# One more pair of input buffers and two more output buffers in the last stage of an attention and two-layer MoE kernel on one core

## The chip, the cores and the metric

The kernel runs on one core of a Trainium2 chip. The metric is the device time of one execution in microseconds (us), the median of the executions shown. Beside it stands one execution taken with the hardware profiler; all rows below come from that one. PE is the matrix engine, PEld its weight loads, DVE the vector engine, ACT the scalar engine, SP the engine that issues nearly all transfers; SPq is its queue.

## The reference, cut to what matters

```python
p_packed = sm_attn(p, k, v)               # 8 x 8 heads, 576 tokens, head size 64, 32 packed rows
out = sm_attn(q, p_packed, p_packed)
x  = out, heads merged                    # 4608 tokens x 512
h  = (x @ w1) * (x @ w2) @ w3             # 512 -> 1024 -> 1024
x2 = h @ w_out                            # 1024 -> 512
g  = leaky(x2 @ moe2_w_in)                # 512 -> 2048, max(0.01 h, h)
y  = g @ moe2_w_out                       # 2048 -> 512
```

All is float32. The kernel computes each large product in three passes: every operand is split into a high part that the matrix engine takes exactly and a low rest, and high x high, high x low and low x high are added in PSUM.

## The kernel before, in words

The first part, up to about 604 us, does the attention and the first MoE layer and leaves x2 in DRAM. The change is in the part behind it, the last stage, which does g and y with Strassen's scheme in Winograd's form: a product of 2 x 2 blocks is made from seven block products instead of eight, and each operand is therefore needed in seven sums of its blocks, its "forms", every one as a high and a low part.

The stage runs over 18 tiles, numbered t (`TB`). The 2048 middle columns are cut into three parts F of width 3, 3 and 2 (`PARTS`, the `n` below), and each part runs over six blocks of 768 tokens (`NB`); t counts through the six blocks of F = 0, then of F = 1, then of F = 2. For a tile:

- `load_forms` (line 664) fetches the seven forms of x2 of that token block from the DRAM buffer `xfd`, two transfers of 384 KB for each, into tiles with the tags `xh` and `xl`. Each tag has `XF` buffers, used in turn. The first four forms of tile t + 1 stand in the program ahead of the output work of tile t - 1, the other three behind it.
- `h_unit` makes x2 @ w_in: for the forms in the order 1, 2, 6, 5, 7, 4, 3, and for each of the n column chunks, 6 matmuls of 384 columns (line 750). So a form is 18 matmuls where n is 3 and 12 where it is 2. The sums in PSUM are taken out by ACT copies (line 710), DVE additions (line 713) and the leaky activation (line 698). PSUM has three banks called b, three c, two a.
- `g_ops` makes the forms of g with ACT casts (line 540) and DVE subtractions (lines 536, 125).
- `begin_o` takes four output tiles with the tag `o`, which has `OB` buffers; for F > 0 it loads the partial result of the part before into each (line 802, 384 KB).
- `o_unit` makes g @ w_out for the tile before, adds into the `o` tiles (lines 708, 713; ACT copies at line 710 where F is 0) and stores the four of them (line 821) to `part` or, for F = 2, to `out`.
- Where a part ends, the weight forms of the next are made: `make_wi` (loads at line 654) and `load_wo` / `make_wo` (line 691), with casts and subtractions at the same lines 540, 536 and 125.
- In tiles 0 to 3 the forms of x2 for the token blocks behind are made beside it (`stage_b`, loads at line 554, stores at 558).

Instructions of one engine run in the order in which they stand in its queue, and a transfer that waits for its buffer holds all that is behind it on SPq. That order isn't written by hand here: the program is planned when it is built, with a simulated timeline (line 891). A transfer's place on SPq, and how the matmuls of `h_unit` and `o_unit` are interleaved, come from when the plan thinks that buffers and operands are ready. Other counts of buffers can so change the order of all engines in this stage.

The pools `b1` (with `xh`, `xl`) and `b2` (with `o`) lie in SBUF where the tiles of the first part lay.

Of the kernel before, what the change touches and what calls it, by code (L numbers as in the profile page):

```python
# [57 lines left out]
def tile_kernel(ctx, tc, qT, kT, vL, pT, w12, w3b, wo1, win, wo2, out):  # L58
# [573 lines left out]
    PARTS = ((0, 3), (6, 3), (12, 2))  # L632
    TB = 3 * NB
    ORDER = (1, 2, 6, 5, 7, 4, 3)
    XF, XR, XT, GR, GS, GH, GL, OB = 4, 5, 2, 5, 2, 5, 5, 4
    wi = {m: b1.tile([P, 2, 2, 384], F32R, name=f"wi{m}") for m in ORDER}

    def form_w(w, size):
# [256 lines left out]
```

## Time and profile before

| what | before |
|---|---|
| median of 3 executions | 1335.64 us (1331.0 to 1338.62) |
| the profiled execution | 1334.15 us |
| its span, first to last instruction | 1332.4 us |
| last stage, first matmul to the end of the span | 604.3 to 1332.4, 728.1 us |
| PE busy, whole span | 1264.0 us (95%) |
| DVE / ACT busy, whole span | 908.5 us (68%) / 623.9 us (47%) |
| transfers, whole span | 283.10 MB, mean 212 GB/s |
| mean granted clock of PE | 0.986 of full speed |

The profiled execution stands 1.5 us below the median and 1.75 us above its own span; a sum that is made in the trace is added to 1334.15. An idle time in the trace is written behind the instruction that ended it, as [idle <- releaser]. Where several things were waited for, the one named is the last by the profile.

### The profile page before, as it was taken

To read this page: it belongs to the slowest core of one execution; us is meant where nothing else is said; L and a number is where in the kernel's file an instruction comes from. 1 tells how busy PE (TensorE), PEld (TensorE's weight loads), DVE (VectorE), ACT (ScalarE), POOL (GpSimd) and SP (SyncE) were. 2 spreads that over 40 slices of the span, in tenths; PEclk is the share of its full clock that TensorE was granted. 3 is DMA by queue.
4 is the path that set the end of the run, shared out by engine and by line. 5 is a ranking of instruction groups with operands and counts; after the bars stand their busy time and mean duration, and the time that the engine had idled before them with its cause. 6 is when DMAs were issued, how large, how long until landed. Compare 5 with 4: busy or idle time off the path is not lost.

```text
span 1332.4 us, 23526 instructions
## 1 busy us (share of the span) xinstructions
PE 1264.0 (95%) x9048; PEld 1187.1 (89%) x9048; DVE 908.5 (68%) x1455; ACT 623.9 (47%) x1165; POOL 138.6 (10%) x105
## 2 busy tenths in 40 slices
PE   5658999999999999999999999989999999999998
PEld 3446989898888989799999999989999999899997
DVE  7999546576767678835867853856576459486667
ACT  4435343545454555535655654645433344344432
POOL 7874101110110101000000000000000000000000
PEclk9779999999999999999999999999999999999999
DMA  9636125384847464626887886366645764878874
GB/s 359 244 125 217 57 77 190 110 292 144 276 147 256 150 223 157 230 99 226 276 316 259 289 287 207 117 237 214 213 149 185 235 213 136 287 257 303 297 288 154
DMA packets 139377, 283.10 MB, mean 212 GB/s; under 512 B 14849, under 2 KB 66049, under 8 KB 139265
## 3 DMA queue, kind: packets, MB, share of 16 engines
q1 hardware_dynamic: 130048, 272.16, 60.1%
q10 hardware_dynamic: 9216, 9.44, 2.1%
q8 instruction: 71, 1.16, 0.4%
q14 instruction: 42, 0.34, 0.1%
HBM read 202.38 MB, written 79.17 MB: 211 GB/s over the span
## 4 chain that ended last, share of the span: by engine, by line
PE 74%; DMA 11%; DVE 8%; issue 3%; POOL 1%; SPq 1%; ACT 1%; POOLq 0%; ACTq 0%; DVEq 0%
PE mm L120 26%; PE b L750 25%; PE c L750 13%; PE a L750 6%; DMA xh<-xfd 4%; PE at L153 3%; DVE cT L269 2%; DMA xl<-xfd 1%; DVE cT L272 1%; DMA part<-o 1%; DMA wi<-wid 1%; PE at L211 1%; DMA xfd<-P 1%; POOL c L279 1%; DMA v<-vL 1%
## 5 line engine op out<-in xcount | busy, mean ns | idle before, releaser
L120 PEld LDWEIGHTS mm<-AT,M 128*128 128x128 f32 x1536 | 207.1, 188 | 31.4 <-issue 10.7
L750 PE MATMUL b<-xh,wi 128*128 128x384 f32 x768 | 219.4, 338 | 11.3 <-DMA xh<-xfd 5.6
L120 PE MATMUL mm<-AT,M 128*128 128x288 f32 x1536 | 223.2, 300 | 5.0 <-DVE W L125 2.3
L750 PE MATMUL b<-gh,wo 128*128 128x384 f32 x768 | 213.8, 335 | 1.4 <-DVE o L713 1.4
L120 PEld LDWEIGHTS mm<-ab,W 128*128 128x128 f32 x1536 | 203.9, 188 | 7.8 <-ACT x2s L455 4.2
L120 PE MATMUL mm<-ab,W 128*128 128x288 f32 x1536 | 207.6, 295 | 0.0
L750 PEld LDWEIGHTS b<-xh,wi 128*128 128x128 f32 x768 | 141.6, 189 | 14.2 <-ACT gr L710 6.1
L750 PEld LDWEIGHTS b<-gh,wo 128*128 128x128 f32 x768 | 140.3, 188 | 2.2 <-issue 1.0
L750 PE MATMUL b<-xl,wi 128*128 128x384 f32 x384 | 129.3, 337 | 0.1
L750 PE MATMUL b<-gl,wo 128*128 128x384 f32 x384 | 128.4, 334 | 0.0
L279 POOL TENSOR_TENSOR c<-cT,c 128x512 int32<-128x512 int32 x56 | 77.1, 1378 | 347.1 <-DVE cT L272 191.2
L750 PE MATMUL c<-gh,wo 128*128 128x384 f32 x384 | 107.3, 336 | 0.8 <-DVE o L708 0.8
L540 ACT CAST gh<-gr 128x1152 fp32r<-128x1152 f32 (+1 forms) x72 | 75.7, 1052 | 69.1 <-PE b L750 32.2
L750 PE MATMUL c<-xh,wi 128*128 128x384 f32 x384 | 106.4, 336 | 1.5 <-DMA xh<-xfd 1.5
L125 DVE TENSOR_TENSOR gl<-gr,gh 128x1152 fp32r<-128x1152 f32 (+1 forms) x72 | 87.7, 1223 | 23.4 <-ACT gh L540 23.3
L120 PE MATMUL mm<-ab,w 128*128 128x512 f32 x192 | 57.1, 454 | 40.8 <-DVE W L125 14.7
L434 DVE TENSOR_TENSOR ab<-mm,a 128x288 f32<-128x288 f32 x128 | 57.7, 453 | 50.2 <-PE mm L120 33.6
L120 PEld LDWEIGHTS mm<-ab,w 128*128 128x128 f32 x192 | 41.0, 220 | 56.1 <-DVE W L125 15.3
L540 ACT CAST gh<-gs 128x1152 fp32r<-128x1152 f32 (+1 forms) x54 | 56.9, 1054 | 61.4 <-PE b L750 32.7
L125 DVE TENSOR_TENSOR ab<-ab,ab 128x288 fp32r<-128x288 f32 x124 | 61.3, 496 | 35.5 <-ACT ab L439 33.7
L698 ACT ACTIVATE gr<-gr 128x1152 f32<-128x1152 f32 (+1 forms) x54 | 57.3, 1062 | 46.0 <-DVE gr L713 45.7
L439 ACT CAST ab<-ab 128x288 fp32r<-128x288 f32 x128 | 55.1, 432 | 45.3 <-DVE ab L434 45.1
(123 smaller groups left out, 2155.4 us busy)
## 6 DMA issues: line engine op xcount, KB each, us to landing
xh<-xfd SPq DMA_DIRECT2D x126, 384.0 KB, 5.4
xl<-xfd SPq DMA_DIRECT2D x126, 384.0 KB, 5.0
part<-o SPq DMA_DIRECT2D x48, 384.0 KB, 2.9
o<-part SPq DMA_DIRECT2D x48, 384.0 KB, 4.2
c<-wo SPq DMA_DIRECT2D x19, 512.0 KB, 5.1
xfd<-xt SPq DMA_DIRECT2D x49, 192.0 KB, 3.2
xfd<-xr SPq DMA_DIRECT2D x49, 192.0 KB, 3.4
raw<-kT SPq DMA_DIRECT2D x32, 288.0 KB, 5.3
```

The lines of the kernel that those rows point to most:

```text
L120: ins = nc.tensor.matmul(dst, lhs(i), rhs(j), start=first and n == 0, stop=last and n == 2)
L125: engine.tensor_tensor(out=out, in0=x, in1=rd(hi), op=ALU.subtract)
L153: ins = nc.tensor.matmul(dst(h)[c * 32:c * 32 + 32], lhs[r, c, :], rhs(c)[r], start=True, stop=True)
L211: ins = nc.tensor.matmul(ps[r, :64], PT[:K, c, r], v[:K, c, g * 64:g * 64 + 64], start=c == 0, stop=c == 4)
L269: in_turn(nc.vector.tensor_scalar(out=t, in0=hw, scalar1=3, scalar2=0x3FFFFFFF, op0=ALU.logical_shift_left, op1=ALU.bitwise_and))
L272: nc.vector.scalar_tensor_tensor(out=t, in0=hw, scalar=0xC0000000, in1=t, op0=ALU.bitwise_and, op1=ALU.bitwise_or)
L279: nc.gpsimd.tensor_tensor(out=q, in0=t.bitcast(I32), in1=q, op=ALU.add)
L434: nc.vector.tensor_tensor(out=t, in0=pb[:, :TH], in1=a, op=ALU.mult)
L439: nc.scalar.copy(t[:, 0], ab32[fc, th])
L540: nc.scalar.copy(hi[step], x[step])
L698: nc.scalar.activation(out=out, in_=x, func=AF.Prelu, alpha=0.01)
L750: nc.tensor.matmul(dst, lhs(l), rhs(r), start=first and n == 0, stop=last and n == total - 1, skip_group_check=True)
```

## The change

Two numbers change. The tags `xh` and `xl` get five buffers each instead of four (`XF`), and the tag `o` gets six instead of four (`OB`). One `xh` or `xl` buffer is 3,072 bytes in each partition and so is an `o` buffer, so each pool grows by 6,144 bytes in each partition; that memory held nothing in this stage. No instruction is added or removed, and no byte more is moved.

```diff
@@ -632,7 +632,7 @@
     PARTS = ((0, 3), (6, 3), (12, 2))
     TB = 3 * NB
     ORDER = (1, 2, 6, 5, 7, 4, 3)
-    XF, XR, XT, GR, GS, GH, GL, OB = 4, 5, 2, 5, 2, 5, 5, 4
+    XF, XR, XT, GR, GS, GH, GL, OB = 5, 5, 2, 5, 2, 5, 5, 6
     wi = {m: b1.tile([P, 2, 2, 384], F32R, name=f"wi{m}") for m in ORDER}
```

## Rows read from the trace of the kernel before

**Rows 1.** Busy time of line 750 in the stage: us, PE and PEld (instructions), clock, DMA.
```profile
604.30:1332.40 728.10, 709.26 (x4032) 701.12 (x4032) 1.00 0.69 235
```

**Rows 2.** Waits of PE from 600 us on: who, for whom, us in total, times, longest.
```profile
PE b L750 <- DMA xh<-xfd: 5.6, 4, 2.5
PE b L750 <- ACT gr L710: 5.2, 3, 3.5
PE c L750 <- DMA xh<-xfd: 1.5, 4, 0.4
PE b L750 <- DVE o L713: 1.4, 2, 0.7
PE c L750 <- DVE o L708: 0.8, 2, 0.5
PE b L750 <- ACT x2s L455: 0.5, 1, 0.5
PE c L750 <- DMA xl<-xfd: 0.3, 2, 0.2
```

**Rows 3.** Timeline of SPq and PE: start, us, instruction, [idle <- releaser].
```profile
810.26 0.43 SPq L821 DMA_DIRECT2D part<-o  x1
810.78 1.24 SPq L664 DMA_DIRECT2D xh<-xfd  x1
...
817.88 0.44 PE L750 MATMUL b<-xh,wi 128*128 128x384 f32 x1 [2.47 <-DMA xh<-xfd]
```

**Rows 4.** Chain of waits from 600 us on: one form's matmuls where n is 3.
```profile
795.52 3.12 PE c L750 x18
```

**Rows 5.** Waits of SPq from 700 us on: for whom, us, times, longest.
```profile
SPq L821 <- DVE o L713: 134.1, 28, 17.8
SPq L664 <- PE b L750: 83.6, 45, 5.6
SPq L802 <- DMA part<-o: 39.6, 19, 5.1
SPq L802 <- DMA out<-o: 33.2, 14, 5.8
```

**Rows 6.** Chain of waits, 870 to 896 us, around the longest wait of PE.
```profile
873.39 4.38 DMA part<-o
...
877.79 0.32 SPq L802
...
878.20 0.39 SPq L691
```

**Rows 7.** Timeline of ACT and PE behind that.
```profile
884.50 0.92 ACT L540 CAST wo<-wo 128x384 fp32r<-128x384 f32 x2 [3.78 <-DMA wo<-wod]
887.47 0.44 PE L750 MATMUL b<-xh,wi 128*128 128x384 f32 x1 [3.48 <-ACT gr L710]
```

**Rows 8.** Busy time in stretches, all lines: PE, PEld, DVE, ACT, POOL, clock, DMA, GB/s.
```profile
814.00:818.00 4.00, 1.44 (x7) 1.13 (x8) 1.11 (x2) 2.34 (x5) 0.00 (x0) 1.00 1.01 361
888.00:892.00 4.00, 4.00 (x16) 4.00 (x15) 4.00 (x10) 2.57 (x6) 0.00 (x0) 0.57 0.98 359
```

**Rows 9.** Chain of waits, 1076 to 1096 us, at the last change of part.
```profile
1079.78 5.73 DMA part<-o
...
1085.53 0.32 SPq L802
...
1086.42 5.05 DMA wi<-wid
...
1091.49 0.40 ACT wi L540
```

**Rows 10.** Waits of ACT from 604.3 us on for weights that were not there.
```profile
ACT wi L540 <- DMA wi<-wid: 17.9, 8, 4.9
...
ACT wo L540 <- DMA wo<-wod: 9.3, 5, 3.8
```

**Rows 11.** Chain of waits at the end, 1296 us on.
```profile
1315.95 3.24 DMA out<-o
...
1319.21 4.32 DMA o<-part
...
1323.62 0.57 DVE o L708
```

**Rows 12.** DMA issues: transfers, KB each, median us from issue to landing.
```profile
xh<-xfd SPq DMA_DIRECT2D x126, 384.0 KB, 5.4
...
part<-o SPq DMA_DIRECT2D x48, 384.0 KB, 2.9
o<-part SPq DMA_DIRECT2D x48, 384.0 KB, 4.2
```

## The prediction, made before the changed kernel was run

> **What bounds the kernel now.** The reader starts with the busy time of the matmuls alone, in the stretch that the change touches [rows 1]. From the stage's first matmul to the end of the span are 728.1 us, and PE is busy for 709.26 of them. So the whole stage has 18.8 us in which PE stands, and nothing that only changes buffers can give back more than that and what a lower clock costs. The work itself does not shrink: 4032 matmuls before and after.
>
> The second view is who PE waits for [rows 2]. The seven rows make 15.3 us; the 3.5 us that are missing to 18.8 lie behind the last matmul. They fall into four kinds: 7.4 us for forms of x2 that had not landed (5.6 + 1.5 + 0.3), 5.2 us for ACT copies out of PSUM, 2.2 us for the DVE additions of the output (1.4 + 0.8), and 0.5 us at the start of the stage, which the change does not touch.
>
> The third view is the queue that issues the transfers, since it decides when a form or a partial result comes [rows 5]. Its longest wait, 134.1 us, is for output that is still being added; a store stands at its head and all loads behind it stand too. 83.6 us are loads of forms that wait for a matmul to free their buffer, and 39.6 + 33.2 = 72.8 us are loads of partial results that wait for the store of the same buffer to land. The change touches the last two kinds and not the first.
>
> **Part one, the fifth pair of form buffers.** It removes no instruction. With four buffers the load of a form can begin when the form four places earlier has been used up; with five, when the form five places earlier has. That is one form of matmuls earlier: 18 of them take 3.12 us [rows 4], two thirds of that in the last part, and more where output matmuls lie between. The largest wait shows what this is worth: the load of a form is issued at 810.78, behind a store at 810.26, and PE stands 2.47 us for it at 817.88 [rows 3]. The longest form wait, 2.5 us, is below 3.12 us, so if every load moved up by one form, all 7.4 us would go. That is the upper end. The lower end of this part is nothing: a load whose buffer is free earlier but which stays behind the same store on SPq lands no earlier. I take 6.0, near the upper end, because the load's place on SPq is planned from when its buffer is free, so with an earlier buffer it should be planned ahead of that store, and because the wait that takes its place is one form later in the order and has 3.12 us of matmuls in front of it.
>
> **Part two, two more output buffers.** With four buffers every load of a partial result waits for the store from the same buffer, one output unit earlier, to land. With six, two of the four loads use buffers whose stores landed a unit earlier; the other two still wait. What it costs PE now is seen at two places. At the longest wait, a store issued at 873.39 takes 4.38 us to land, the load of a partial result behind it can go only at 877.79, and behind that load stands the one of the output weights, at 878.20 [rows 6]. ACT waits 3.78 us for these weights with a cast; copies out of PSUM stand behind that cast, and PE waits 3.48 us for one of them [rows 7]. At the last change of part it is the same with the input weights: store 5.73 us, load at 1085.53, weights issued at 1086.42 and landed 5.05 us later, ACT goes on at 1091.49 [rows 9], and PE loses most of what remains of the 5.2 us in [rows 2]. The bounds of this term are 0 (if the plan leaves a still waiting load ahead of the weights) and 5.2. I take 4.0.
>
> The clock adds a little to it. Behind the 3.48 us wait the granted clock is 0.57 for 4 us, close to the lower level of 1.2 GHz, and 16 matmuls run in 4.00 us [rows 8]; at 3.12 / 18 = 0.173 us they would take 2.8. So that wait costs 1.2 us more. Behind the 2.47 us wait the clock was still 1.00 [rows 8]. Bounds 0 and 1.2, taken 1.0, with the wait that causes it.
>
> At the end of the kernel the last partial result is loaded at 1319.21, after the store from its buffer that went at 1315.95, and takes 4.32 us; DVE adds into it at 1323.62 and the last matmuls wait for banks [rows 11]. The waits for DVE are 2.2 us in the whole stage [rows 2], and I count them all to this place, which is an upper end. With six buffers the two last loads may still wait for the first two stores of the unit before, so I take 1.0 between 0 and 2.2. The 3.5 us behind the last matmul (a DVE addition and a store to land) stay.
>
> **What is added.** The loads come earlier by up to a form and the plan of the stage is made anew. No row shows the new order, so its cost is bounded from both sides. On the low side it may be below nothing, since a new order can also lose small waits; I see no more than the 0.5 us at the start of the stage for that. On the high side stands the worst that the trace shows of a plan that was wrong on the chip: ACT waits 17.9 + 9.3 = 27.2 us for weights that the plan thought landed [rows 10], and 5.2 of these reach PE now; if all did, it would be 22.0 more. I take 3.5, nearer to the low side: about half of the 7.4 us of form waits come back at other places, because none of these waits is longer than 2.5 us and the plan cannot know a landing time that closely.
>
> The two pools also lie at other addresses. Where a tile of the stage lies over a tile of the first part that is still in use, its first load waits. The first tile has 0.5 us of such waiting in [rows 2], and the stage's first forms were there in time; I cost it at nothing, covered by the matmuls of the first part, and at some 3 us (a form's matmuls, [rows 4]) if that cover fails.
>
> **The sum.** -6.0 - 4.0 - 1.0 - 1.0 + 3.5 = -8.5 us. From the profiled execution's 1334.15 that is 1325.65, given as 1326. Against the median, 1335.64, it is 0.7% less. All upper ends together would be -7.4 - 5.2 - 1.2 - 2.2 - 0.5 = -16.5, so 1318.
>
> **The rivals.** (a) *A transfer that is early only pushes another.* In 888 to 892 us the DMA engines are busy 0.98 of the time at 359 GB/s [rows 8], and a form lands in 5.4 us where a store of the same size takes 2.9 [rows 12]. In such a stretch a load that is issued earlier takes the time from one that is issued behind it. Against it: over the whole stage the share is 0.69 [rows 1], so there is room between the stretches. Half of the 12.0 gained would then be given back: 1334.15 - 6.0 + 3.5 = 1331.7, given as 1332. The Trainium skill (DMA: Bandwidth & Descriptors, Issuing engines are not separate DMA queues) says the like: all transfers run on the same 16 DMA engines and interleave, whoever issues them. The trace agrees in the 0.98 share of that stretch.
>
> (b) *The loads stay behind the stores.* SPq stands 134.1 us at stores that wait for DVE [rows 5], and no buffer of this change ends those. If the plan leaves the loads where they are, PE's waits stay too: 1334 to 1336. For it speaks that the largest form wait had a store at its head [rows 3]; against it, that the buffer is what the plan asks for first.
>
> (c) *Slower: ACT is stopped more often by weights.* The plan sees buffers free earlier, moves the loads of weights and the casts on them forward, and ACT stands at a cast whose weights are still in flight while copies that PE needs stand behind it. Its place is the two changes of part. Its price is known: 3.48 us of PE and 1.2 of clock at one, 1.5 at the other [rows 7, 8]. Of the 13 waits of ACT for weights [rows 10] three or four more of the long kind, at 4.7 us each, outweigh the 12.0 us gained: at four it is 1334.15 - 12.0 + 18.8 = 1341, and it decides from the third on. Against it: this change frees SPq just there, so the weights should come earlier.
>
> **How the numbers follow.** The forecast of 1326 gets 0.50, (a) 0.19, (b) 0.18, (c) 0.13. The forecast's own range is 1318 to 1331, from the bounds above. The range that should hold the time 8 times in 10 takes in (a) and (b), and the near half of (c) beyond them: 1318 to 1338. About 0.5% is what a measurement of this kernel can tell from no change, 6.7 us, so faster means below 1329 and slower above 1342.3. Of the forecast 0.45 lie below 1329, of (a) 0.05: faster 0.50. Of (c) about 0.10 lies above 1342: slower 0.10. The rest, 0.40, is the same.
>
> **What would show it.** In the profile of the changed kernel PE's waits for forms should fall from 7.4 us to about 3, and those for ACT copies from 5.2 to about 1. On SPq the waits of partial-result loads for stores should fall from 72.8 us to half or less, those of form loads for matmuls may stay, since a fifth buffer is also filled and then waited for. The lower clock behind 888 us should be gone. Busy time of PE must stay near 709 us. The prediction is wrong if PE's waits for forms stay above 6 us (part one does nothing), if ACT's waits for weights grow beyond 27.2 us and reach PE (rival c), or if landing times of forms rise well above 5.4 us (rival a).

## The result and the profile after

The changed kernel takes 1318.64 us (median of 4 executions, 1317.17 to 1321.55) where the kernel before takes 1335.36 on the same chip; the ratio is 0.988, 95% interval 0.985 to 0.991. The forecast was 1326 with a range of 1318 to 1338: the direction is right, the median lies 0.6 us above the lower end of the range, and the gain is 16.7 us where 8.5 were summed. The profiled execution took 1317.17 us, the lowest of the four; its span is 1315.4 us, 17.0 less than before.

The busy time of line 750 in the stage of the changed kernel, with the columns of [rows 1]:

```profile
601.90:1315.40 713.50, 703.48 (x4032) 699.97 (x4032) 1.00 0.69 239
```

Against [rows 1] three things differ. The stage starts 2.4 us earlier (601.9 for 604.3). It is 14.6 us shorter (713.5 for 728.1). And PE is busy for 703.48 us and not 709.26, with the same 4032 matmuls; the prediction had held that number fixed.

The waits of PE in the changed kernel from 590 us on, with the columns of [rows 2]; these are all of them:

```profile
PE b L750 <- DVE o L708: 1.6, 2, 0.9
PE c L750 <- DMA xh<-xfd: 1.5, 2, 0.8
PE c L750 <- DVE o L708: 0.9, 2, 0.6
PE b L750 <- DVE gl L125: 0.7, 1, 0.7
PE b L750 <- DVE o L713: 0.7, 1, 0.7
PE b L750 <- ACT gr L710: 0.5, 1, 0.5
PE b L750 <- ACT x2s L455: 0.5, 1, 0.5
PE b L750 <- ACT o L710: 0.4, 1, 0.4
```

They make 6.8 us where [rows 2] make 15.3. Waits for forms went from 7.4 to 1.5, those for copies of ACT out of PSUM from 5.2 to 0.9. Waits for DVE's work on outputs rose from 2.2 to 3.2, and 0.7 for the subtraction of a form of g is new. The 0.5 us for ACT's x2s lies ahead of the first matmul, in both kernels, and so outside the stretches above.

The timeline of SPq beside [rows 3], in the changed kernel:

```profile
790.79 0.56 SPq L664 DMA_DIRECT2D xh<-xfd  x1
791.39 0.60 SPq L664 DMA_DIRECT2D xl<-xfd  x1
...
797.81 2.05 SPq L821 DMA_DIRECT2D part<-o  x3
```

These two loads fetch the fifth form of tile 5, in front of the stores at 797.81. In [rows 3] the load of the same form came at 810.78, behind the same four stores, and PE stood 2.47 us for it. That is the step of part one as it was meant.

The stretches where the low clock was, to be held against the second row of [rows 8]:

```profile
884.00:888.00 4.00, 4.00 (x25) 4.00 (x25) 2.80 (x5) 2.35 (x4) 0.00 (x0) 1.00 0.99 346
888.00:892.00 4.00, 4.00 (x25) 4.00 (x24) 3.08 (x3) 2.95 (x5) 0.00 (x0) 1.00 0.77 253
```

The clock is 1.00 and PE is full in both. DMA is as busy in the first (0.99) as it was in [rows 8].

The waits of SPq from 700 us on, with the columns of [rows 5]:

```profile
SPq L821 <- DVE o L713: 152.9, 25, 19.8
SPq L664 <- PE b L750: 64.4, 38, 4.5
...
SPq L802 <- DMA part<-o: 36.0, 22, 4.1
...
SPq L802 <- DMA out<-o: 20.3, 12, 3.4
```

Loads of partial results still stand 56.3 us for stores (72.8 before). The forecast had asked for half or less.

### The profile page after: what moved, and what is told of

The parts are those of the page before. It is cut to its first block, busy times and chain, and to the rows that moved or that the text cites. A ratio compares the mean times of both kernels' runs of the same rounds, so it can differ in the third digit from the quotient of the medians.

```text
span 1315.4 us, 23515 instructions
## 1 busy us (share of the span) xinstructions
PE 1258.2 (96%) x9048; PEld 1186.4 (90%) x9048; DVE 910.3 (69%) x1455; ACT 621.8 (47%) x1165; POOL 138.2 (11%) x105
## 4 chain that ended last, share of the span: by engine, by line
PE 81%; DVE 8%; DMA 7%; issue 3%; ACT 1%; POOL 0%; SPq 0%; DVEq 0%; ACTq 0%; POOLq 0%
PE mm L120 32%; PE b L750 25%; PE c L750 12%; PE a L750 6%; PE at L153 4%; DVE cT L269 2%; DMA xfd<-xr 2%; DVE cT L272 1%; DMA xfd<-xt 1%; DMA xh<-xfd 1%; DVE gl L125 1%; PE at L211 1%; DMA wi<-wid 1%; DMA xr<-x2d 1%; PE at L192 1%
```

## The experiments

The two parts alone come first, then what the run with the changed kernel could not tell apart. Edits are on the kernel before where nothing else is said; each gain is against the kernel before on the same chip.

**The fifth pair alone.**

```diff
-    XF, XR, XT, GR, GS, GH, GL, OB = 4, 5, 2, 5, 2, 5, 5, 4
+    XF, XR, XT, GR, GS, GH, GL, OB = 5, 5, 2, 5, 2, 5, 5, 4
```

> Five buffers for the forms, four for the output as before. Theory A (each part does its own: the fifth pair ends the waits for forms, the output buffers end the waits behind weights): PE's waits for forms fall from 7.4 us to about 2, the 3.48 us wait for an ACT copy and the low clock behind it stay, so some 1335.4 - 8.3 = 1327 us. Theory B (the fifth pair alone does it, as forms that come early also take the load off the queue): 1319 us, the long ACT wait gone. Theory C (the new addresses and the new order of the plan do it, whatever buffers are there): about half, 1327 us, but then the run with empty memory in place of the buffers gives the like.

Measured: 1322.23 us, ratio 0.990 (0.988 to 0.992), 13.5 us faster. The time lies between A and B, nearer to B. The waits of PE, the largest:

```profile
PE c L750 <- DMA xh<-xfd: 2.2, 2, 1.2
PE b L750 <- DVE o L708: 1.6, 2, 0.9
PE b L750 <- ACT o L710: 1.6, 1, 1.6
...
PE c L750 <- ACT gr L710: 0.4, 1, 0.4
```

Waits for forms are 2.8 us (with 0.6 in two rows left out). The 3.48 us wait for an ACT copy and the low clock behind it are gone, with four output buffers, as B said; a new wait of 1.6 us for another ACT copy stands at 791 us. So the two output buffers are not needed to end the long wait.

**The output buffers alone.**

```diff
-    XF, XR, XT, GR, GS, GH, GL, OB = 4, 5, 2, 5, 2, 5, 5, 4
+    XF, XR, XT, GR, GS, GH, GL, OB = 4, 5, 2, 5, 2, 5, 5, 6
```

> Six buffers for the output, four for the forms as before. Theory A: the waits of PE for ACT copies at the two changes of part fall from 5.2 us to about 1 and the low clock goes, the form waits stay at 7.4: 1335.4 - 6 = 1329 us. Theory B: 1335 us, nothing. Theory C: between the two, about 1327 us.

Measured: 1334.74 us, ratio 0.999 (0.997 to 1.001), no change that can be told. PE's waits and SPq's:

```profile
PE b L750 <- ACT gr L710: 5.5, 3, 3.0
PE b L750 <- DMA xh<-xfd: 3.5, 3, 2.0
```

```profile
SPq L802 <- DMA part<-o: 40.1, 17, 4.9
SPq L802 <- DMA out<-o: 33.9, 12, 6.8
```

The waits for ACT copies are all there (5.5 for 5.2), and loads of partial results stand 74.0 us for stores, where [rows 5] make 72.8. Waits for forms are 4.6 us in this profile (7.4 in the one before), but 1.7 for a form's subtraction is new and the clock is low at three places, so the time is the same. Theory A falls for this part: two more buffers took away neither of the waits that they were meant for.

**Empty memory in place of the buffers.**

```diff
-    wi = {m: b1.tile([P, 2, 2, 384], F32R, name=f"wi{m}") for m in ORDER}
+    wi = {m: b1.tile([P, 2, 2, 384], F32R, name=f"wi{m}") for m in ORDER}; b1.tile([P, 1536], F32, name="pad1")
...
-    part = dram.tile([2, DM, NT], F32, name="part")
+    part = dram.tile([2, DM, NT], F32, name="part"); b2.tile([P, 1536], F32, name="pad2")
```

> The buffers of the kernel before, with an unused tile of 6,144 bytes in each partition in each of the two pools, so that the tiles lie at other addresses and the pools are as large as in the changed kernel. Theory A and B: within 3 us of before, 1333 to 1336 us, with the waits of before; if the 2.4 us by which the first matmul of the last stage came earlier in the changed kernel is due to the addresses, it shows here too. Theory C: 1327 us or less.

Measured: 1331.88 us, ratio 0.997 (0.995 to 0.999). It is 3.8 us faster with no buffer more. The waits for forms (6.5 us) and for ACT copies (4.2) stayed. So theory C does not carry the gain, but a part of it: see the run on the pool's reach.

**Loads of partial results on another queue.**

```diff
-                    nc.sync.dma_start(out=o, in_=part[F - 1, r, c0:c0 + UT].rearrange("p (j c) -> p j c", j=2))
+                    nc.gpsimd.dma_start(out=o, in_=part[F - 1, r, c0:c0 + UT].rearrange("p (j c) -> p j c", j=2))
```

> The buffers of the kernel before; only the loads of partial results are issued from GpSimd's queue instead of SyncE's. So they still wait for the stores of their buffers, but hold nothing else up. Theory A (the cost of four output buffers is that the waiting load holds the queue): the waits for ACT copies behind weights go as in the run with six output buffers, 1329 us. Theory B: 1335 us. If the wait for the partial result itself was the cost, PE's waits for DVE grow and it is 1335 us or more.

Measured: 1336.62 us, ratio 1.001 (0.999 to 1.003). PE's longest waits:

```profile
PE b L750 <- DMA xh<-xfd: 7.7, 6, 2.4
PE c L750 <- DVE o L708: 2.4, 2, 2.0
PE c L750 <- DMA xh<-xfd: 1.8, 2, 1.5
```

The waits for ACT copies into `gr` did fall, from 5.2 to 0.5 (0.7 for a copy into `o` is new). But waits for forms rose from 7.4 to 9.5, those for DVE's additions into the output from 2.2 to 4.1, 2.7 us for DVE's additions into `gr` are new, and nothing was won. This profile is also a long one of its kernel, 1341.73 us.

It looks as if A were right about the ACT waits: take the waiting load out of the queue, and the weights come. The rows of SPq between 876 and 882 us say otherwise, first what it waited for and then the issue that followed:

```profile
SPq L691 <- PE a L750: 4.0, 1, 4.0
880.91 0.37 SPq L691 DMA_DIRECT2D wo<-wod  x1
```

With no load of a partial result on SPq, the last transfer of output weights still stood 4.0 us, now for matmuls that read the old weights in the same place. It went 4.2 us behind the third store of its tile; in [rows 6] it was 4.8 us (873.39 to 878.20). So the load of the partial result had cost these weights 0.6 us and not 4.4. What else shortened ACT's wait here (the transfer took 4.6 us to land instead of 6.3, and one more copy stands in front of the cast) isn't separated.

**The changed kernel and the fifth pair alone, side by side.** The first is the changed kernel as it is, the second the edit `XF` = 5 alone.

> The changed kernel as it is, five buffers for the forms and six for the output, so that it stands beside the run with the fifth pair alone on the same chip. Theory D (the output buffers are worth something only behind the fifth pair): 1318 to 1320 us and at least 2.5 us below the fifth pair alone. Theory E (they are worth nothing, the 3.6 us between the two so far come from the chips and runs): within 1.5 us of it.

> Five buffers for the forms, four for the output, once more, beside the changed kernel. Theory D: 1322 us, 2.5 us or more above the changed kernel. Theory E: within 1.5 us of it.

Measured: 1319.56 us, ratio 0.989 (0.987 to 0.991), and 1321.42 us, ratio 0.991 (0.989 to 0.993). The difference is 1.9 us here and was 3.6 us between the first runs of the two. Both have the same sign, neither stands clear of the intervals, and 1.9 is between what D and E asked for. Whether the output buffers are worth 2 to 4 us behind the fifth pair, or nothing, stays open. The profiled executions show how much one program varies: the waits for forms were 3.6 us in this profile of the changed kernel and 1.5 in the first. One of them is followed by the low clock again (the second row has the columns of [rows 8]):

```profile
1221.10 0.41 PE L750 MATMUL c<-xh,wi 128*128 128x384 f32 x1 [2.08 <-DMA xh<-xfd]
1222.00:1226.00 4.00, 4.00 (x16) 4.00 (x15) 0.56 (x1) 0.00 (x0) 0.00 (x0) 0.57 0.77 250
```

**The pool's reach.** The memory of the stage's first pool, with `wi`, `xh` and `xl`, ends below the tiles that feed the first layer's M units; by the sizes of the tiles in the kernel, 6,144 bytes more in it reach past that. Here only the pool's end moves, no tile that is used.

```diff
-    slots(last, fill, spread(stage_b(2, 1), 11, 23))
+    slots(last, fill, spread(stage_b(2, 1), 11, 23)); b1.tile([P, 1536], F32, name="pad1")
```

> The kernel before; only an unused tile of 6,144 bytes in each partition is taken from the first pool after all others, so that no tile that is used lies elsewhere, but the pool's end reaches into the memory of the pool with the weights of the first layer. Theory F (the stretch in front of the last stage got shorter because the pool that reaches into those weights opens only when they are done with, so the sums of the w_in forms no longer come in between the first layer's own work on DVE and ACT): the stretch from the second M unit to the first matmul of the stage falls from 66.6 to about 63 us, and the time to 1332, as with empty memory in both pools. Theory G (it is the addresses of the tiles): 66.6 us and 1335.

Measured: 1334.14 us, ratio 0.999 (0.997 to 1.001), so no change of time that can be told; but the stretch changed as F said. The timelines of PE and DVE, of before and then of this run: the first M unit of the last batch (line 153), the first sum of the w_in forms (line 536), the first matmul of the stage.

```profile
537.71 1.09 PE L153 MATMUL at<-w,ppT 64*32 64x512 f32 x16
539.00 0.55 DVE L536 TENSOR_TENSOR xr<-wi,wi 128x384 f32<-128x384 f32 x1
604.33 0.45 PE L750 MATMUL b<-xh,wi 128*128 128x384 f32 x1 [0.49 <-ACT x2s L455]
```

```profile
540.61 1.09 PE L153 MATMUL at<-w,ppT 64*32 64x512 f32 x16
569.85 0.55 DVE L536 TENSOR_TENSOR xr<-wi,wi 128x384 f32<-128x384 f32 x1
603.52 0.44 PE L750 MATMUL b<-xh,wi 128*128 128x384 f32 x1 [0.49 <-ACT x2s L455]
```

The stretch is 604.33 - 537.71 = 66.6 us before and 62.9 here, and the sums of the w_in forms start 31 us later. In before three waits of PE lie in it that are not here, 2.5 us in all; the two longest:

```profile
553.78 1.08 PE L120 MATMUL mm<-AT,M 128*128 128x288 f32 x6 [0.47 <-DVE ab L434]
556.54 1.06 PE L120 MATMUL mm<-AT,M 128*128 128x288 f32 x6 [1.68 <-ACT a L428]
```

All nine profiles of kernels whose first pool reaches past that point, the changed one among them, have 62.9 or 63.0 us; the five others have 65.0 to 68.2. So the 3.7 us are real in their stretch, and they come from the pool's size, not from a tile's address (theory G) and not from the buffers. In the time of a whole execution they are hard to see: the stretch begins at 537.1 to 541.1 us from profile to profile, which is as much as its gain. The stage's first matmul is at 602.1 us in the mean of the nine profiles and at 604.6 in that of the five. (The expectation calls this unit the second M unit; it is the first of the four.)

**Three pairs.** `XF` = 3, `OB` = 4.

> Three buffers for the forms, four for the output. If it is the one form of matmuls more or less in stock that makes PE wait for forms, a buffer less takes 3.12 us from each load's lead: PE's waits for forms rise from 7.4 us to 25 or more and the time to 1355 us. If the gain of the fifth pair came from a luckier order of the plan, it can go either way, and stays within 10 us of before, 1326 to 1345 us.

Measured: 1358.6 us, ratio 1.018 (1.015 to 1.021).

```profile
PE c L750 <- DMA xh<-xfd: 14.7, 7, 5.2
PE b L750 <- ACT gr L710: 3.4, 3, 2.9
PE b L750 <- DMA xh<-xfd: 2.8, 3, 2.2
```

Waits for forms are 18.1 us (with 0.6 for `xl`), less than the 25 expected, and the time is 23 us longer, outside what the theory of a luckier order allowed (1326 to 1345). Only about half of it is in named waits (27 us for 15); the rest is busy time, with the low clock at several places.

**Eight output buffers.** `XF` = 4, `OB` = 8.

> Four buffers for the forms, eight for the output. In the order of the queue, each load of a partial result with six buffers stands where the load two places earlier stood with four, and with eight where the load four places earlier stood: as many loads wait behind as many stores, only for a later tile. Theory H (so more output buffers free nothing): 1335 us within 4, SPq's waits of these loads for stores 70 to 78 us. Theory I (six were too few, a whole unit ahead would do): 1329 us or less, these waits below 40 us.

Measured: 1334.08 us, ratio 0.999 (0.997 to 1.001). The loads' waits for stores are 39.9 + 26.6 = 66.5 us, a little under theory H's 70. Why the buffers bring nothing here can be read from the order of SPq's instructions in the three programs. For each load of a partial result, in order, the number of output stores that stand ahead of it on SPq:

```
four buffers:   22 23 23 24 26 27 28 28 30 30 32 32 34 34 35 36 ...
six buffers:    20 20 22 23 23 24 26 27 28 28 30 30 32 32 34 34 ...
eight buffers:  20 20 20 20 22 23 23 24 26 27 28 28 30 30 32 32 ...
```

Over all 48 loads, the lists are the same but for a start of two or four loads (and one count of 46 for 47). The plan puts a load in the queue when it thinks that a buffer comes free. With more buffers it is the load of a later tile that stands there, and it waits for the same store.

**Six pairs.** `XF` = 6, `OB` = 4.

> Six buffers for the forms, four for the output. With one form's matmuls more in front of each load than with five, PE's waits for forms should fall from some 3 us to below 1.5; the rest of PE's waits stay. 1319 to 1322 us, against 1322 with five. If the waits for forms stay at 3 us, the queue and not the buffers holds them, and it is 1322.

Measured: 1319.11 us, ratio 0.987 (0.985 to 0.989). PE waits for no form any more; what is left, 6.6 us with the start, is for ACT and DVE, the largest:

```profile
PE c L750 <- DVE o L708: 1.8, 2, 1.6
PE b L750 <- ACT o L710: 1.4, 1, 1.4
PE b L750 <- DVE o L708: 1.1, 2, 0.7
PE c L750 <- ACT gh L540: 1.1, 1, 1.1
```

So six pairs with four output buffers are as fast as the change. They also went as expected (1319 to 1322 us, form waits below 1.5).

**Stores on another queue.** On the changed kernel:

```diff
-            nc.sync.dma_start(out=todo[x][1], in_=todo[x][0])
+            (nc.sync if t == TB - 1 else nc.gpsimd).dma_start(out=todo[x][1], in_=todo[x][0])
```

> The changed kernel; the output stores of all tiles but the last are issued from GpSimd's queue, which is empty in this stage, instead of SyncE's. SPq stood 153 us at stores that waited for DVE; if these still hold up loads that PE waits for, the 1.5 to 3.6 us of form waits go: 1316 us. If loads only meet the same stores as waits for their buffers: 1319 us. If the loads move ahead of what they collide with now, or a store from that queue takes longer to land and the output buffers come free later: 1322 us or more.

Measured: 1318.50 us, ratio 0.987 (0.985 to 0.989), as the changed kernel. From 700 us on SPq stood 198 us at stores in the changed kernel, 153 of them in the first row shown above; here it is 12.6. Its loads of partial results stand 186.6 us for stores, where it was 56.3, and its loads of forms and weights stand 220 us for matmuls, where it was 147. So the waits went to other rows, and the time stayed.

**Both.** Six pairs, four output buffers and the stores on GpSimd's queue.

> Six buffers for the forms, four for the output, and the output stores of all tiles but the last from GpSimd's queue: the two edits that came out best, together. If what is left of PE's waits is only the ends of additions and copies, the two give nothing on top of each other: 1317 to 1320 us. If the stores still held up loads of forms, 1315 us.

Measured: 1324.15 us, ratio 0.993 (0.991 to 0.996), slower than either edit alone, against both expectations. Its profile (1321.06 us, the lowest of its executions) has one wait of a new size, near the end, for an addition into an output whose partial result came late:

```profile
PE c L750 <- DVE o L708: 4.3, 2, 3.6
PE b L750 <- ACT gr L710: 2.4, 2, 2.2
```

What makes the other executions 3 us longer than that was not looked into. No version was found that beats the changed kernel by more than the runs can tell.

## Why the prediction came out as it did

**What bounds the stage.** The waits of PE were the right view, but the ceiling made of them was too low. The prediction held that nothing can give back more than the 18.8 us in which PE stands and what a low clock costs, and that busy time stays near 709 us. The stage lost 14.6 us: 8.8 of idle time (18.8 to 10.0) and 5.8 of busy time (709.26 to 703.48). So 5.8 us came from where it counted only 1.0, for the clock. A matmul's record lasts 0.33 us while the next one starts 0.173 us behind it: where PE runs without a stop the records overlap, and at each stop one of them counts in full. The matmul behind the stop also starts late, at 818.16 after 817.88. From start to start the row that says 2.47 costs 2.74. By starts, 4032 matmuls at 0.173 us need 697.4 us, and the stage had 26.6 us above that before and 12.0 after. The clock's part was 1.5 us: about ten matmuls behind 888 us start 0.32 us apart.

The piece behind the last matmul is 3.8 us in both kernels; the prediction's 3.5 comes of counting the 0.5 us ahead of the first matmul into the stage. And the first row of [rows 8] ends where the 2.47 us wait does, so it can't tell of the clock behind it; in 818 to 822 us that is 1.00 too.

**Part one** was right in cause: the fifth pair ends most waits for forms, and at the largest wait the load moved ahead of the stores as said. The size, 6.0 between 0 and 7.4, is at the top of what was measured: these waits fell by 5.9 in the first profile, by 3.8 in the repeat, and by 4.6 and 3.6 with the fifth pair alone. With three pairs they are 18.1 us, with four 4.6 to 9.5 in six profiles (kernels with another edit among them), with five 1.2 to 3.8 in five, and with six 0 and 0.5. But part one was priced by these waits alone, and the fifth pair alone gained 13.5 and 14.2 us.

**Part two** had the right size and the wrong cause, so its size is luck. The waits for ACT copies fell by 4.3 where 4.0 was taken. But the long ones go with the fifth form pair alone (2.0 and 0.8 us are left) and stay with six or eight output buffers alone (5.5 and 6.0 us). Two steps failed. One says that two of the four loads would no longer wait: they would not if the order on SPq stayed, but it is planned from the buffers, and each freed buffer was given to a load of a later tile (72.8 us of these waits before, 74.0 with six buffers). The other is the price: it charged PE's wait to the load of a partial result that holds the weights in the queue, and that load held the last of them for 0.6 us. They could not go earlier than the last matmul that reads the old weights, which in the kernel before is

```profile
877.23 0.34 PE L750 MATMUL b<-gh,wo 128*128 128x384 f32 x1
```

The timeline of SPq, in the run with the fifth pair alone:

```profile
867.26 0.37 SPq L691 DMA_DIRECT2D wo<-wod  x1
```

The last transfer of output weights goes at 867.26 there, and at 878.20 in [rows 6]. Before, the output unit of tile 5 still had work from 875.84 to 877.57, in the middle of the second form of tile 6 (begun at 873.93); with the fifth pair it is finished at 867.6, before that form starts at 869.7. So these weights come 11 us earlier because the output unit is done earlier, in the order that comes with the fifth pair. Why the plan orders it so (because a form more is in stock) is an inference; that the wait goes with the fifth pair is shown.

**The clock**, taken at 1.0 of at most 1.2: it had cost 1.5, and it is 1.00 where it was 0.57. It went there with the wait in front of it. It isn't gone for good: in the second profile of the changed kernel it is 0.57 behind a wait of 2.08 us for a form, longer than any left in the first.

**The end of the kernel**, taken at 1.0: 0.4 came. PE waits 0.65 us twice in the changed kernel's last four microseconds of matmuls, where it waited 1.66 in all before; and PE's waits for DVE's work on outputs rose by 1.0 in the stage as a whole.

**What is added**, taken at 3.5: new waits for DVE, the output additions 1.0 and the form subtraction 0.7, 1.7 us in all. The direction was right, the size twice too large; it was argued that half of the old form waits come back at other places, and what came were waits for DVE.

**The other addresses** were costed at nothing with 3 us as a loss, and no gain was allowed for. That bound failed. The pool's reach shortened the stretch in front of the stage by 3.7 us, and the stage started 2.4 us earlier in the first profile (2.5 in the means above). The two runs that have it without any buffer are 1.4 and 3.8 us faster in the median, and only the second is clear of no change.

So the sum, 8.5, was 8.5 us too small against the 17.0 of the profiled execution: 4.8 us of busy time beyond the 1.0 for the clock, 2.4 at the start of the stage, 0.8 in the last two terms of the sum taken together (2.5 us of loss, where 1.7 came), and 0.5 in waits for forms, copies and short stops.

**The rivals.** (a) did not happen: a form (`xh`) still lands in 5.4 us and the DMA share is the same 0.69. (The 0.98 share behind 888 us was reached with transfers of SPq alone, so it shows full engines and nothing of who issues.) (b) is what part two did, alone: the loads stay behind the stores, and the lists of the run with eight output buffers show how. It is not what part one did. (c) did not happen: ACT still waits 17.9 + 12.8 = 30.7 us for weights, more than the 27.2 that the prediction named as a warning, but only 0.9 us of copies reach PE. The second half of that test, "and reach PE", is what counts.

## What to carry to other kernels

Where an engine stands for operands that come late, a buffer more is worth one step of work in front of each load; compare that step (here 3.12 us) with the longest wait (2.5 us) and try one more and one fewer, to see where it ends. The comparison alone said here that every form wait would go, and 1.2 to 3.8 us stayed. Where a load waits for a store and the queue's order is planned from free buffers, more buffers can move the wait to a later load instead of ending it, so count in the queue's order what stands ahead of each load. Where a transfer goes late behind a waiting one, ask what it would have waited for itself: here that left 0.6 us. And try the memory empty: a pool that grows can change the order of other work.

## What the runs showed that was not expected

The busy time of PE is not the work: 4032 equal matmuls took 709.26, 704.86 and 703.48 us of it before, with the fifth pair alone and after, the less the fewer stops there are (1.5 us of the first is the low clock). The distance from start to start, 0.173 us, gives the time above the work. And moving a wait off a queue moved it elsewhere: without its stores SPq stood 186.6 us instead of 56.3 at the loads that need them, and the time was the same.
